# Sliding-window attention with a spectral mix on one core: the last rows of Yw and the jobs under the last loads

## The chip, the core and the metric

The kernel runs on one core of a Trainium2 chip. The metric is the device time of one execution in microseconds (us). The engines are PE (TensorE; PEld is its weight load), DVE (VectorE), ACT (ScalarE), POOL (GpSimd) and SP (SyncE), which only issues transfers here. SPq, ACTq and POOLq are the queues of an engine that issues a transfer.

## What is computed

Batch is 8, there are 8 heads of 64, 576 tokens, and a model width of 512. Attention looks back over 64 tokens; its result x then goes through a spectral mix: a real FFT over the tokens, two 512 x 512 matrices for each of the lowest 64 modes, the inverse FFT, a residual and a channel product with a relu.

```
x  = softmax(mask(q @ k.T / 8)) @ v            # heads side by side: [8, 576, 512]
X  = rfft(x, axis=1)                           # the first 64 modes are kept
Yr = Xr @ w_r[m] - Xi @ w_i[m]
Yi = Xr @ w_i[m] + Xi @ w_r[m]                 # for each mode m
u  = x + irfft(Y)
out = u + max(u @ w_ch, 0)                     # float32
```

## The kernel before

**Stages.** First comes attention, batch by batch, with the forward transform as matmuls (XQ holds the spectra). Meanwhile POOL already issues the loads of the 64 modes' matrices, 512 KB each, which run until about 398 us. The modes are worked off in groups of four (`mode_half`, L167 to L185: half of the input width, w_r or w_i). Each group gives rows of Y, which are turned so that they lie in `Yall` (128 rows: 64 real, 64 imaginary; 8 batches; 512 columns).

**The algebra of the end.** u is x plus the inverse transform of Y, and u @ w_ch is x @ w_ch plus the inverse transform of Y @ w_ch. So two tables of rows are kept: `Yall` (Y, bfloat16) and `Zall` (Yw = Y @ w_ch, fp32r). Each output tile of 128 tokens and 512 columns needs u, from x and a matmul of the table `trigI` with `Yall` (`yrows(b)`), and z, from `XW` = x @ w_ch and a matmul of `trigIr` with `Zall` (`zrows(b)`). There are 36 tiles: four per batch in `x_sb` (stored as [128, 2 halves, batch, 4 tiles, 256]) and four in `x4`, each of which joins the last 64 tokens of two batches and is sent as two outputs of 64 partitions.

**Jobs under the loads.** `jobs` is a list of pairs (prepare, done). `advance()` (L607) runs the next job's prepare and then the done of the job before it. The main loop (L807 to L863) runs one `mode_half`, then as many jobs as a count `want` allows; in the last halves these are 24 jobs spread over six halves. Before the last half but one it drains the list (L827). `batch_job(b)` (L670) turns the rows of a batch (DVE L673, PE L676, ACT L677) and multiplies them by `wch` (PE L604), and DVE casts the result to `zrows(b)` (L681). `early_job(b, c)` (L687), for the first four batches (NLB = 4) and each of their four tiles, adds z of the rows known so far into `XW` (PE L693, DVE L694) and makes an early sum of u called `UE`: for odd c in a spare place of XQ, by DVE (L698, L700); for even c in the place of x itself, by ACT (L702, L703, L705). The order of the jobs is a batch, its four tiles in the order 1, 0, 3, 2, the next batch, and at the end the four batches that have no early sums.

**The last rows.** The last two groups of modes (`LAST`, 16 rows) come after the early sums. Their rows of Y and Yw go two ways: as `YL` and `ZL`, small operands that are added onto the early sums (`late_u`, `late_z`, L752 to L764), and through `yst` and `zst` by SP's queue into `Yall` and `Zall` (L884, L895), for all tiles without early sums.

**The outputs.** `seq` (L728 to L734) is a list of 18 pairs of tiles. The eight AA pairs have early sums: PE adds XW and the late rows, DVE adds the late u (`take_u`, L775), ACT takes the relu (L781), POOL adds the two (L782), and the tile is sent. The ten BB pairs (`full`, L785) have none: PE adds x by an identity matmul (L789) and the rows of `Yall` (L740), ACT copies u (L792), PE does the same for z (L746, L740), and DVE takes the relu and adds (L796). The order is three AA pairs, then BB and AA in turn, then the rest of BB; the first two BB pairs are x4 tiles. Even and odd places of `seq` use different PSUM banks. The results lie in `ut`, a ring of seven pairs. `send` (L766) issues the outputs on SP's queue in the order of the program, with every other one on ACT's queue in the last two pairs.

```
banks_u(0); late_u(0); take_u(0)
pz = ...                                  # L890: the last rows of Y times wch
late_z(0); take_z(0)                      # sends the outputs of pair 0
nc.vector.tensor_copy(out=zst, in_=pz)
nc.sync.dma_start(out=Zall...[rows], in_=zst...)
```

Of the kernel before, what the change touches and what calls it, by code (L numbers as in the profile page):

```python
# [9 lines left out]
FP32 = mybir.dt.float32  # L10
# [16 lines left out]
def kernel(  # L27
# [163 lines left out]
    with tc.manual_schedule():  # L191
# [478 lines left out]
        def batch_job(b):  # L670
            def prepare():
                tr = trpool.tile([128, NDCH, 128], FP32R, name="tr")
                nc.vector.tensor_copy(out=tr, in_=YT[:, b])  # L673
                pt = bank("t", [128, NDCH, 128], BF16, "ptx")
                for c in range(NDCH):
                    nc.tensor.transpose(out=pt[:, c, :], in_=YT[:, b, c, :], identity=ident_bf)  # L676
                nc.scalar.copy(out=yrows(b), in_=pt.rearrange("p c e -> p (c e)"))  # L677
                return tr

            def done(tr):  # L680
                nc.vector.tensor_copy(out=zrows(b), in_=multiply(tr))  # L681

            jobs.append((prepare, done))

        UE = {}

        def early_job(b, c):  # L687
            i = 9 * (b // 2) + 4 * (b % 2) + c
            tokens = slice(128 * c, 128 * c + 128)

            def done(_):
                pz = bank("z")
                nc.tensor.matmul(out=pz, lhsT=trigIr[:, tokens], rhs=zrows(b), start=True, stop=True)  # L693
                nc.vector.tensor_tensor(out=XW[i], in0=pz, in1=XW[i].bitcast(FP32), op=ALU.add)  # L694
                pu = bank("t")
                halves = pu.rearrange("p (h e) -> p h e", h=2)
                if c % 2:
                    nc.tensor.matmul(out=pu, lhsT=trigI[:, tokens], rhs=yrows(b), start=True, stop=True)  # L698
                    UE[i] = spare[2 * b + c // 2].rearrange("p (h e) -> p h e", h=2)
                    nc.vector.tensor_tensor(out=UE[i], in0=halves, in1=tiles[i][0], op=ALU.add)  # L700
                else:
                    nc.tensor.matmul(out=halves, lhsT=ident_bf, rhs=tiles[i][0], start=True, stop=False)  # L702
                    nc.tensor.matmul(out=pu, lhsT=trigI[:, tokens], rhs=yrows(b), start=False, stop=True)  # L703
                    UE[i] = x_sb[:, :, b, c:c + 2, :].rearrange("p h c e -> p h (c e)").bitcast(FP32)
                    nc.scalar.copy(out=UE[i], in_=halves)  # L705

            jobs.append((lambda: None, done))


        tiles = []  # L710
        for kk in range(B // 2):
            for b in (2 * kk, 2 * kk + 1):
                tiles += [(x_sb[:, :, b, c, :], [(128 * c, b)], [out[b, 128 * c:128 * c + 128, :]]) for c in range(NTC - 1)]
            tiles.append((x4[:, :, kk, :], [(576, 2 * kk), (512, 2 * kk + 1)], [out[2 * kk + i, 512:576, :] for i in range(2)]))
        NT = len(tiles)
        XW = {}

        def x_jobs(pl, lo, hi):
# [9 lines left out]
        AA = [(18 * k // 2 + c, 18 * k // 2 + 4 + c) for k in range(NLB // 2) for c in range(4)]  # L728
        BB = [(8, 17), (26, 35)] + [(i, i + 1) for k in range(NLB // 2, B // 2) for i in range(9 * k, 9 * k + 8, 2)]
        assert sorted(i for p in AA + BB for i in p) == list(range(NT))  # L730
        seq = [AA.pop(0) for _ in range(3)]
        while AA:
            seq += [BB.pop(0), AA.pop(0)]
        seq += BB  # L734
# [37 lines left out]

        def take_u(n):
            for i in seq[n]:
                nc.vector.tensor_tensor(out=UE[i], in0=pu[i].rearrange("p (h e) -> p h e", h=2), in1=UE[i], op=ALU.add)  # L775

        def take_z(n):
            ut = ringA.tile([128, 2, DM], FP32, name="ut", tag="wt")
            for j, i in enumerate(seq[n]):
                rt = ut[:, j].rearrange("p (h e) -> p h e", h=2)  # L780
                nc.scalar.activation(out=ut[:, j], in_=ps[i], func=ACT_F.Relu)  # L781
                nc.gpsimd.tensor_tensor(out=rt, in0=UE[i], in1=rt, op=ALU.add)  # L782
                send(i, ut[:, j], n)

        def full(n):  # L785
            banks_u(n)
            ut = ringA.tile([128, 2, DM], FP32, name="ut", tag="wt")
            for j, i in enumerate(seq[n]):
                nc.tensor.matmul(out=pu[i].rearrange("p (h e) -> p h e", h=2), lhsT=ident_bf, rhs=tiles[i][0],  # L789
                                 start=True, stop=False)  # L790
                add_rows(pu[i], i, trigI, yrows, False)
                nc.scalar.copy(out=ut[:, j], in_=pu[i])  # L792
            tail_xw(n)
            for j, i in enumerate(seq[n]):
                add_rows(ps[i], i, trigIr, zrows, False)
                nc.vector.scalar_tensor_tensor(out=ut[:, j], in0=ps[i], scalar=0.0, in1=ut[:, j],  # L796
                                               op0=ALU.max, op1=ALU.add)
                send(i, ut[:, j], n)
# [8 lines left out]
        for i, (grp, hb) in enumerate(steps[EARLY:]):  # L807
            f, l = grp < EARLY or hb == 0, hb == 1
            if i == EARLY:
                while tables:  # L810
                    tables.pop(0)()
                while jobs or pend:
                    advance()
                close(stmp2, yp, ringB)
                Zall = pool("zall", side="right").tile([2 * NM, B, DM], FP32R, name="Zall")
                x_jobs(pool("xp1", side="right", reuse_waits="tile"), NX0, NT)
                nc.vector.memset(YT[:, :, :, rows], 0.0)
                nc.vector.tensor_scalar(out=trz.rearrange("p c g k -> p c (g k)"), scalar1=0.0, scalar2=None, op0=ALU.mult,
                                        in0=ident.unsqueeze(1).to_broadcast([128, NDCH, 128]))
                for g in range(4):  # L820
                    nc.sync.dma_start(out=trigL[32 * g:32 * g + 16], in_=trigI[rows, 0:512])
                    nc.sync.dma_start(out=trigLr.bitcast(FP32)[32 * g:32 * g + 16], in_=trigIr.bitcast(FP32)[rows, 0:512])
                given = 0
            if f:
                psm = bank("m")
            for ri in range(2):
                if half == n0 + n1 - 2:  # L827
                    while jobs or pend:
                        advance()
                if half == n0 + n1 - 1:  # L830
                    late["warm"], late["zeros"] = bank("z"), trigI[:, 0:DM]
                    keep_warm(5)
                    late["first"] = bank("z")
                    late[0][1]()
                    tail_xw(0)
                mode_half(psm, grp, hb, ri, f, l)
                load_weights(len(wlist))
                while ready:
                    ready.pop(0)()
                for t in tables[0:2]:  # L840
                    t()
                del tables[0:2]
                if half == 0:
                    nc.gpsimd.dma_start(out=wch, in_=moe_w_ch.rearrange("(c p) e -> p c e", p=128))
                if l and ri:
                    finish_group(grp, psm)
                    if grp == NGRP - 1:
                        ready.pop(0)()
                        for b in range(B):
                            batch_job(b)  # L850
                            if b < NLB:
                                for c in (1, 0, 3, 2):
                                    early_job(b, c)
                half += 1
                if half <= n0:
                    want = max(half - 4, 0) * NX0 // (n0 - 4)
                elif half <= n0 + n1 - 8:
                    want = (half - n0) * (NT - NX0) // (n1 - 8)
                else:
                    want = NT - NX0 + (half - n0 - n1 + 8) * (B + 4 * NLB) // 6  # L860
                while given < want:
                    advance()
                    given += 1  # L863
# [12 lines left out]
        for c in range(NDCH):  # L876
            nc.tensor.matmul(out=zl, lhsT=trz[:, c].rearrange("p g k -> p (g k)"), rhs=wch[:, c, :],
                             start=(c == 0), stop=(c == NDCH - 1))
        put_y()
        take()  # L880
        nc.vector.tensor_copy(out=ZL, in_=zl)
        yst = rowpool.tile([128, DM], BF16, name="yst")
        nc.scalar.copy(out=yst, in_=late["py"])
        nc.sync.dma_start(out=Yall[rows], in_=yst)  # L884
        banks_u(0)
        late_u(0)
        take_u(0)
        pz = bank("p")
        for c in range(NDCH):
            nc.tensor.matmul(out=pz, lhsT=tr[:, c, :], rhs=wch[:, c, :], start=(c == 0), stop=(c == NDCH - 1))  # L890
        zst = trpool.tile([128, NDCH, 128], FP32R, name="tr").rearrange("p c k -> p (c k)")
        late_z(0)
        take_z(0)
        nc.vector.tensor_copy(out=zst, in_=pz)
        nc.sync.dma_start(out=Zall.bitcast(FP32)[rows], in_=zst.bitcast(FP32))  # L895
        for n in range(1, len(seq)):
            if seq[n][0] in UE:
                tail_xw(n)
# [39 lines left out]
```

## Time and profile before

| | |
|---|---|
| runs shown | 448.43 us median of 3 (448.31 to 448.49) |
| the profiled execution | 448.99 us, of which the span from the first to the last instruction is 447.2 us |
| busy, share of the span | PE 76%, DVE 53%, PEld 48%, ACT 40%, POOL 32% |
| loads of the weights | 82 MB on POOL's queue, 211 GB/s |
| outputs | 38 on SP's queue and 2 on ACT's; 256 KB each, eight of them 128 KB |
| tail (last weights landed to the end) | about 398 to 447.2 us |

Three things help to read it. A share of busy time is a mean over stages with different limits; what a change in one stage is worth is read from that stage. The page's second part cuts the span into 40 slices of 11.2 us, each digit a busy share in tenths, and gives the clock that PE was granted and what the transfers moved. The line of an instruction in the order of time ends with how long its engine had been idle before it, and what ended that.

### The profile page before, as it was taken

How to read it: one execution, taken by the hardware profiler on the slowest of the kernel's cores; microseconds unless marked ns; L12 is line 12 of the kernel's file. 1: busy time of each engine (PE TensorE's matmuls, PEld its weight loads, DVE VectorE, ACT ScalarE, POOL GpSimd, SP SyncE). 2: the span in 40 equal slices, each digit the busy share in tenths (PEclk: the TensorE clock that was granted, in tenths of full speed). 3: DMA queues.
4: the chain of work that ended last, by engine and by line, in shares of the span. 5: the costliest groups of instructions: out<-in, count | busy, mean ns of one | idle time of the engine just before them, and what ended most of it. 6: DMA issues, size and time to landing. Idle time of an engine off the chain costs nothing. (4 is left out here: it accounts for less than half of the span.)

```text
span 447.2 us, 11052 instructions
## 1 busy us (share of the span) xinstructions
PE 337.8 (76%) x4720; PEld 214.0 (48%) x4765; DVE 234.9 (53%) x476; ACT 176.8 (40%) x315; POOL 142.9 (32%) x211
## 2 busy tenths in 40 slices
PE   6888899998999978974254565576866688796885
PEld 3666767676667665641032232343433343343443
DVE  8688787876676754863022111131322158735475
ACT  5665757575757563522001011121222122314363
POOL 9332323333233233232322322222232223106460
PEclk9999999999999998986569676798899899999799
DMA  8999999999999999999999999999999999933787
GB/s 203 210 212 210 211 211 210 211 211 213 210 211 211 211 211 210 211 211 211 235 233 218 211 211 211 211 211 211 211 211 211 211 211 211 211 65 99 210 292 282
DMA packets 48129, 93.65 MB, mean 209 GB/s; under 512 B 3664, under 2 KB 3856, under 8 KB 48080
## 3 DMA queue, kind: packets, MB, share of 16 engines
q0 software_dynamic: 42000, 81.73, 96.9%
q1 hardware_dynamic: 5792, 10.69, 7.3%
q8 instruction: 37, 0.61, 0.5%
q10 hardware_dynamic: 288, 0.52, 0.3%
q14 instruction: 12, 0.10, 0.1%
HBM read 163.58 MB, written 9.44 MB: 387 GB/s over the span
## 5 line engine op out<-in xcount | busy, mean ns | idle before, releaser
L158 POOL DMA_DIRECT2D wi<-in_moe_w_i_dram x62 | 44.0, 710 | 96.6 <-PE psm L178 41.3
L722 DVE CAST xw<-psz 128x512 fp32r<-128x512 f32 x36 | 24.9, 691 | 87.5 <-PE psz L604 84.6
L604 PE MATMUL psz<-wch,tr 128*128 128x512 f32 x176 | 59.1, 466 | 11.0 <-DMA wch<-in_moe_w_ch_dram 11.0
L158 POOL DMA_DIRECT2D wr<-in_moe_w_r_dram x53 | 37.8, 714 | 88.5 <-PE psm L178 40.2
L276 DVE TENSOR_REDUCE mx<-s 128x4 fp32r<-128x512 f32 x72 | 49.5, 688 | 26.3 <-PE s L272 26.0
L578 ACT CAST tr<-ptx 128x512 fp32r<-128x512 bf16 x36 | 21.1, 587 | 100.7 <-PE ptx L597 100.7
L178 PEld LDWEIGHTS <-XQ 128*32 128x32 bf16 x448 | 20.7, 166 | 77.0 <-issue 69.0
L178 PE MATMUL psm<-wi,XQ 128*32 128x512 bf16 x212 | 28.3, 461 | 31.1 <-DMA wi<-in_moe_w_i_dram 30.8
L286 ACT ACTIVATE p<-s 128x512 bf16<-128x512 f32 x72 | 39.7, 603 | 12.9 <-PE s L284 12.9
L604 PEld LDWEIGHTS psz<-wch,tr 128*128 128x128 f32 x176 | 34.9, 220 | 17.5 <-issue 11.5
L178 PE MATMUL psm<-wr,XQ 128*32 128x512 bf16 x180 | 25.1, 482 | 22.8 <-DMA wr<-in_moe_w_r_dram 22.8
L272 PE MATMUL s<-kT,qT 64*64 64x128 bf16 (+1 forms) x576 | 29.1, 221 | 6.7 <-issue 6.7
L229 ACT COPY kT<-tr 128x576 bf16<-128x576 bf16 x32 | 23.1, 723 | 24.4 <-PE tr L225 24.3
L295 DVE COPY pts<-pt 128x1024 bf16<-128x1024 bf16 (+1 forms) x40 | 25.2, 630 | 8.6 <-PE pt L292 7.3
L229 ACT COPY qT<-tr 128x576 bf16<-128x576 bf16 x32 | 23.3, 728 | 10.4 <-PE tr L225 10.4
L272 PEld LDWEIGHTS <-qT 64*64 64x64 bf16 x576 | 17.8, 107 | 18.0 <-issue 17.5
L284 PE MATMUL s<-mx,ident_r 128*128 128x512 f32 x72 | 26.2, 437 | 0.0
L229 ACT COPY vT<-tr 128x576 bf16<-128x576 bf16 x32 | 23.3, 727 | 4.1 <-PE tr L225 4.0
L292 PE MATMUL pt<-ident_bf,p 128*128 128x128 bf16 x288 | 23.8, 223 | 1.3 <-issue 1.1
L623 DVE TENSOR_TENSOR stg<-psm,Ypair 128x512 bf16<-128x512 f32 x10 | 6.9, 689 | 32.4 <-PE psm L178 32.4
L324 DVE TENSOR_TENSOR x_sb<-o,r 128x512 bf16<-128x512 f32 x32 | 22.1, 691 | 1.1
L225 PE MATMUL tr<-ident_bf,rawk 64*64 64x64 bf16 x576 | 15.4, 196 | 6.2 <-DMA rawk<-in_k_dram 4.8
(194 smaller groups left out, 604.0 us busy)
## 6 DMA issues: line engine op xcount, KB each, us to landing
wi<-in_moe_w_i_dram POOLq DMA_DIRECT2D x60, 512.0 KB, 15.9
wr<-in_moe_w_r_dram POOLq DMA_DIRECT2D x53, 512.0 KB, 16.2
out_dram<-ut SPq DMA_DIRECT2D x30, 256.0 KB, 2.3
rawv<-in_v_dram POOLq DMA_DIRECT2D x16, 288.0 KB, 14.8
rawk<-in_k_dram POOLq DMA_DIRECT2D x15, 288.0 KB, 15.1
rawq<-in_q_dram POOLq DMA_DIRECT2D x15, 288.0 KB, 14.1
Ypair<-in_moe_w_r_dram POOLq DMA_DIRECT2D x5, 512.0 KB, 15.1
x_sb<-in_moe_w_r_dram POOLq DMA_DIRECT2D x4, 512.0 KB, 15.3
```

Source lines behind the costliest of these rows:

```text
L158: nc.gpsimd.dma_start(out=w[:, 0:len(ps)], in_=src[ps[0]:ps[-1] + 1, HALF * hb:HALF * hb + HALF, :].rearrange("g (p j) e -> p g j e", j=NJ))
L178: nc.tensor.matmul(out=psm[32 * g:32 * g + 32, :], lhsT=of.rearrange("k s b m -> k (s b) m")[:, (3 * j + 1 - ri) * B:(3 * j + 5 - ri) * B, ...
L229: nc.scalar.copy(out=to, in_=pt.rearrange("p j n -> p n j"))
L272: nc.tensor.matmul(out=s[ro, t, lo:128], lhsT=lq, rhs=kT[ro, 64 * n - 64 + lo:64 * n + 64], start=False, stop=True, skip_group_check=True)
L276: nc.vector.tensor_reduce(out=mx, in_=s, axis=AX.X, op=ALU.max, negate=True)
L284: nc.tensor.matmul(out=s, lhsT=ident_r, rhs=mx.unsqueeze(2).to_broadcast([128, 4, 128]), start=False, stop=True, skip_group_check=True)
L286: nc.scalar.activation(out=p[:, 4 * c2:4 * c2 + 4, :], in_=s, func=ACT_F.Exp, scale=EX_SCALE)
L292: nc.tensor.transpose(out=pt[:, t, :], in_=st[u]["p"][:, t, :], identity=ident_bf)
L295: nc.vector.tensor_copy(out=ps[:, 0:nt, :], in_=pt[:, 0:nt, :])
L324: nc.vector.tensor_tensor(out=xo.rearrange("p c (h d) -> p c h d", d=64), in0=ov[:, :, :, 0:64], in1=rb, op=ALU.mult)
L604: nc.tensor.matmul(out=pz, lhsT=tr[:, c, :], rhs=wch[:, c, :], start=(c == 0), stop=(c == NDCH - 1))
L722: nc.vector.tensor_copy(out=XW[i], in_=multiply(tr))
```

## The change

It has four parts.

1. **Jobs.** The cast to `zrows(b)` goes from DVE to ACT. `early_job` is split in two kinds: `add_late(b, c)` (z into XW) and `early_u(b, cs)` (the early sum of u). Per batch these are seven jobs, in the order u of tile 1, z of 0, u of 3, z of 1, z of 2, u of 0 and 2 together, z of 3. They are queued behind the batch job of the next batch. So 36 jobs are spread over the six halves.
2. **Early sums in rows of their own.** For tiles 0 and 2 `UE` lies in one half of the batch's place in `x_sb` (one contiguous stretch of 512 float32), no longer in two tiles of both halves. The adds that use UE take it flat.
3. **x by halves.** `full` adds the rows of `Yall` first, and then x by two identity matmuls of 256 columns, one for each half.
4. **The last rows of Yw.** put_y comes behind the cast of ZL in the program, the product with wch (`pz`) ahead of `late_u(0)`; `late_z(0)` ahead of the copy to `zst`, which goes from DVE to ACT; and its transfer to `Zall` ahead of `take_u(0)` and `take_z(0)`, and so of every output. `seq` starts with four AA pairs and not three.

```
             def done(tr):
-                nc.vector.tensor_copy(out=zrows(b), in_=multiply(tr))
+                nc.scalar.copy(out=zrows(b), in_=multiply(tr))
...
-        def early_job(b, c):
...
+        def add_late(b, c):
             def done(_):
+                i = tile_of(b, c)
                 pz = bank("z")
+                nc.tensor.matmul(out=pz, lhsT=trigIr[:, 128 * c:128 * c + 128], rhs=zrows(b), start=True, stop=True)
                 nc.vector.tensor_tensor(out=XW[i], in0=pz, in1=XW[i].bitcast(FP32), op=ALU.add)
             jobs.append((lambda: None, done))
+
+        def early_u(b, cs):
+            def done(_):
+                pus = [bank("t") for _ in cs]
+                for c, pu in zip(cs, pus):
+                    i = tile_of(b, c)
+                    halves = pu.rearrange("p (h e) -> p h e", h=2)
+                    if c % 2 == 0:
+                        nc.tensor.matmul(out=halves, lhsT=ident_bf, rhs=tiles[i][0], start=True, stop=False)
+                    nc.tensor.matmul(out=pu, lhsT=trigI[:, 128 * c:128 * c + 128], rhs=yrows(b), start=(c % 2 == 1),
+                                     stop=True)
+                for c, pu in zip(cs, pus):
+                    i = tile_of(b, c)
+                    if c % 2:
+                        UE[i] = spare[2 * b + c // 2]
+                        nc.vector.tensor_tensor(out=UE[i].rearrange("p (h e) -> p h e", h=2),
+                                                in0=pu.rearrange("p (h e) -> p h e", h=2), in1=tiles[i][0], op=ALU.add)
+                    else:
+                        UE[i] = x_sb[:, c // 2, b].rearrange("p c e -> p (c e)").bitcast(FP32)
+                        nc.scalar.copy(out=UE[i], in_=pu)
+            jobs.append((lambda: None, done))
+
+        def early_jobs(b):
+            early_u(b, (1,))
+            add_late(b, 0)
+            early_u(b, (3,))
+            add_late(b, 1)
+            add_late(b, 2)
+            early_u(b, (0, 2))
+            add_late(b, 3)
...
-        seq = [AA.pop(0) for _ in range(3)]
+        seq = [AA.pop(0) for _ in range(4)]
...
-                nc.tensor.matmul(out=pu[i].rearrange("p (h e) -> p h e", h=2), lhsT=ident_bf, rhs=tiles[i][0],
-                                 start=True, stop=False)
-                add_rows(pu[i], i, trigI, yrows, False)
+                add_rows(pu[i], i, trigI, yrows, True)
+                for h in range(2):
+                    nc.tensor.matmul(out=pu[i][:, HALF * h:HALF * h + HALF], lhsT=ident_bf, rhs=tiles[i][0][:, h],
+                                     start=False, stop=True, skip_group_check=True)
...
                         for b in range(B):
                             batch_job(b)
-                            if b < NLB:
-                                for c in (1, 0, 3, 2):
-                                    early_job(b, c)
+                            if 0 < b <= NLB:
+                                early_jobs(b - 1)
...
-                    want = NT - NX0 + (half - n0 - n1 + 8) * (B + 4 * NLB) // 6
+                    want = NT - NX0 + (half - n0 - n1 + 8) * (B + 7 * NLB) // 6
...
-        put_y()
         take()
         nc.vector.tensor_copy(out=ZL, in_=zl)
+        put_y()
         yst = rowpool.tile([128, DM], BF16, name="yst")
         nc.scalar.copy(out=yst, in_=late["py"])
         nc.sync.dma_start(out=Yall[rows], in_=yst)
-        banks_u(0)
-        late_u(0)
-        take_u(0)
         pz = bank("p")
         for c in range(NDCH):
             nc.tensor.matmul(out=pz, lhsT=tr[:, c, :], rhs=wch[:, c, :], start=(c == 0), stop=(c == NDCH - 1))
+        banks_u(0)
+        late_u(0)
+        late_z(0)
         zst = trpool.tile([128, NDCH, 128], FP32R, name="tr").rearrange("p c k -> p (c k)")
-        late_z(0)
+        nc.scalar.copy(out=zst, in_=pz)
+        nc.sync.dma_start(out=Zall.bitcast(FP32)[rows], in_=zst.bitcast(FP32))
+        take_u(0)
         take_z(0)
-        nc.vector.tensor_copy(out=zst, in_=pz)
-        nc.sync.dma_start(out=Zall.bitcast(FP32)[rows], in_=zst.bitcast(FP32))
```

More of the change, by code (lines that the diff above doesn't have):

```diff
@@ L680, in done @@
             def done(tr):
-                nc.vector.tensor_copy(out=zrows(b), in_=multiply(tr))
+                nc.scalar.copy(out=zrows(b), in_=multiply(tr))
             jobs.append((prepare, done))
         UE = {}
-        def early_job(b, c):
-            i = 9 * (b // 2) + 4 * (b % 2) + c
-            tokens = slice(128 * c, 128 * c + 128)
+        def add_late(b, c):
             def done(_):
+                i = tile_of(b, c)
                 pz = bank("z")
-                nc.tensor.matmul(out=pz, lhsT=trigIr[:, tokens], rhs=zrows(b), start=True, stop=True)
+                nc.tensor.matmul(out=pz, lhsT=trigIr[:, 128 * c:128 * c + 128], rhs=zrows(b), start=True, stop=True)
@@ L694, in done @@
                 nc.vector.tensor_tensor(out=XW[i], in0=pz, in1=XW[i].bitcast(FP32), op=ALU.add)
[L695 to L705, printed above, removed]
@@ L715, with tile_of @@
         NT = len(tiles)
+        def tile_of(b, c):
+            return 9 * (b // 2) + 4 * (b % 2) + c
         XW = {}
@@ L774, in take_u @@
             for i in seq[n]:
-                nc.vector.tensor_tensor(out=UE[i], in0=pu[i].rearrange("p (h e) -> p h e", h=2), in1=UE[i], op=ALU.add)
+                nc.vector.tensor_tensor(out=UE[i], in0=pu[i], in1=UE[i], op=ALU.add)
         def take_z(n):
@@ L779, in take_z @@
             for j, i in enumerate(seq[n]):
-                rt = ut[:, j].rearrange("p (h e) -> p h e", h=2)
                 nc.scalar.activation(out=ut[:, j], in_=ps[i], func=ACT_F.Relu)
-                nc.gpsimd.tensor_tensor(out=rt, in0=UE[i], in1=rt, op=ALU.add)
+                nc.gpsimd.tensor_tensor(out=ut[:, j], in0=UE[i], in1=ut[:, j], op=ALU.add)
                 send(i, ut[:, j], n)
```

## The prediction

> **What bounds the kernel now.** I read the page's slices first, then the busy time of the engines per stretch of the end, the waits from 380 us on, the order of time there, and last the chain.
>
> ```profile
> span 447.2 us, 11052 instructions
> ...
> PE   6888899998999978974254565576866688796885
> ...
> PEclk9999999999999998986569676798899899999799
> ...
> GB/s 203 210 212 210 211 211 210 211 211 213 210 211 211 211 211 210 211 211 211 235 233 218 211 211 211 211 211 211 211 211 211 211 211 211 211 65 99 210 292 282
> ```
>
> Until slice 35 (about 391 us) the weights stream at 211 GB/s without a gap: nothing that only shortens work under them is worth its length. Behind them comes a tail of some 47 us. Its stretches (columns: length, busy us and count of PE, PEld, DVE, ACT, POOL; granted clock; DMA share; GB/s):
>
> ```profile
> 408.00:410.00 2.00, 1.95 (x11) 0.89 (x8) 1.61 (x3) 2.00 (x5) 2.00 (x3) 1.00 0.35 131
> 410.00:412.00 2.00, 0.15 (x1) 0.00 (x0) 0.00 (x0) 0.37 (x1) 2.00 (x3) 1.00 0.66 196
> 412.00:414.00 2.00, 0.00 (x0) 0.00 (x0) 0.00 (x0) 0.00 (x0) 2.00 (x2) 0.57 1.05 222
> 414.00:416.00 2.00, 1.67 (x4) 1.38 (x5) 0.36 (x1) 0.00 (x0) 0.24 (x1) 0.50 0.95 365
> 416.00:418.00 2.00, 2.00 (x8) 0.82 (x8) 1.20 (x3) 0.00 (x0) 0.00 (x0) 0.50 0.24 53
> ...
> 417.60:420.20 2.60, 2.60 (x12) 1.19 (x9) 1.29 (x2) 1.89 (x4) 1.51 (x2) 0.71 0.91 195
> 422.80:425.20 2.40, 1.70 (x8) 1.18 (x9) 0.65 (x2) 1.57 (x4) 2.22 (x2) 1.00 0.96 206
> 438.00:444.00 6.00, 4.62 (x20) 2.67 (x19) 4.27 (x7) 3.01 (x6) 0.00 (x0) 1.00 1.03 381
> ```
>
> PE stops at 410.15, its clock halves, and it comes back at half clock until 419. The waits and the order of time name the causes:
>
> ```profile
> PE psz L740 <- DMA Zall<-tr: 4.2, 1, 4.2
> ...
> PE psy L789 <- DVE x_sb L775: 2.8, 2, 1.5
> ```
>
> ```profile
> 406.82 2.52 POOL L782 TENSOR_TENSOR ut<-x_sb,ut 128x512 f32<-128x512 f32 x2 [21.48 <-ACT ut L781]
> ...
> 410.06 0.59 SPq L895 DMA_DIRECT2D Zall<-tr  x1
> ...
> 414.33 2.07 PE L740 MATMUL psz<-Zall,trigIr 128*128 128x512 f32 x4 [4.18 <-DMA Zall<-tr]
> ```
>
> The last rows of Yw (Zall) stand in SP's queue behind the first two outputs, which wait for POOL. The second wait is of another kind: L789 reads x of batches 4 to 7, L775 writes UE in batches 0 to 3; nothing is shared but the interval from one half of x_sb to the other. It occurs behind the two L775 that write x_sb (423.50, 430.67) and behind none that writes XQ, so I take it as false. The chain begins with that very wait and then runs through PE:
>
> ```profile
> 430.02 0.61 DVE x_sb L775
> 430.63 0.05 issue
> 430.68 0.39 PE psy L789
> ```
>
> Before the tail, under the loads, the batch jobs go round from cast to cast of Zall in 6.12 us, and end at the last L178 but one:
>
> ```profile
> 366.10 0.69 DVE L681 CAST Zall<-psz 128x512 fp32r<-128x512 f32 x1 [0.25 <-PE psz L604]
> ...
> 372.22 0.69 DVE L681 CAST Zall<-psz 128x512 fp32r<-128x512 f32 x1 [0.69 <-PE psz L604]
> ...
> 395.93 0.66 PE L178 MATMUL psm<-wr,XL 128*32 128x512 bf16 x8
> ```
>
> **Step 1: jobs under the last loads.** Their end (395.93) decides when the tail starts: the last four loads land at 393.0, 395.4, 396.7 and 398.0 (issue plus time to landing) and are used 2.6 to 3.0 us later. So at most 2.6 us can be won here; every us lost counts whole. Now a round is: cast 0.69, z matmul to its add 0.53, five DVE adds 0.61 apart (3.05), L673 0.41, multiply to cast 1.23: 5.9, measured 6.12. After: the cast is on ACT and batch b's adds come behind the multiply of b+1, so none waits for a fresh cast: multiply 1.02 on PE, first u matmul to add 0.41, five adds 3.05, L673 0.41: 4.9. Three rounds save 3.1. Against it: PE's slack shrinks, and of the three half-modes that fall in these rounds (each 0.38 issue and 0.59 work) I let two stand on the path, 1.9. Net **-1.2**. ACT's eight casts (L578, the same form, 587 ns: 4.7 us) lie in its idle time: ACT is busy some 9 of 33 us here, and if L677 delayed them all, 0.6 a round, the gain would be gone. More jobs per half (6 for 4) are the same instructions, cut finer. Bounds of the step: -2.6 to +1.0.
>
> **Step 2: Zall ahead.** Times on the old clock. put_y ends at 404.05, the four L890 matmuls (1.20) at 405.25, ACT's copy (0.58, behind yst, which ended at 404.85) at 405.9, SP issues at once, ahead of any output. Landing lies between that of Yall's rows (3.1 us) and the old one behind outputs (4.2): 409.1 to 410.2. take_u(0) starts 1.3 us later on DVE, at 405.9, since late_u follows L890; but POOL needs the relu too, which ends at 406.75 as before, and DVE's first add ends at 406.6. POOL still starts at 406.8: the first output does not move. PE then has three more AA pairs, 1.05 us each beside ACT's relus, to 409.2, then the first BB pair (x4): u matmuls 1.3, xw 0.47, first use of Zall at 411.0. **No wait**: 4.2 us off PE, and no idle stretch long enough for the clock to fall (4.8 us of work at 0.50, worth 2.4).
>
> **Step 3: x by halves, UE in rows of its own.** The two false waits held PE 1.27 and 1.50 us idle. One 512-column matmul becomes two of 256, on 20 tiles. The trace has none of 256; four transposes of 128 take 0.23, a 512 takes 0.22, so in proportion nothing, and at worst one uncovered weight load of 0.10 a tile, 2.0 in all. I take nothing: PE will not be last. A flat UE costs the same (POOL: 1270 ns for the x_sb form, 1280 for XQ).
>
> **PE's end.** First BB pair to 411.9; four AA at 1.25, 5.0; the second x4 pair 2.7; eight BB at 1.80 (434.99 to 436.79 is one): 14.4. It ends at 434.0, before at 442.67; with the 4.5 us from there to the span's end, 438.5.
>
> **What is late next: the outputs.** SP sends in the order of the program, so BB0 leaves behind AA3, and AA's outputs come from POOL at 1.26 each, now without a break from 406.82: AA3's first at 415.6. From there 26 full outputs and 8 half ones are left. Full ones moved at 381 GB/s (438 to 444): 0.69 each, 17.9. Half ones (64 partitions, 128 KB) moved 512 KB in 2.5 us in both stretches shown (195 and 206 GB/s at a full DMA share): 0.63 each, 5.0. POOL and PE supply four in 2.5 and 3.0 us, DMA needs 2.8 and for an x4 pair more, so it hardly pauses. Last landing 415.6 + 2.0 + 22.9 - 0.7 = 439.9, and 1.2 to the span's end as before: 441.1. That is later than PE's 438.5, so the tail wins **6.1**, not 8.7. [...]
>
> **Sum.** Span 447.2 - 1.2 - 6.1 = 439.9. The profiled execution took 448.99 with 1.79 outside its span, and lies 0.56 above the median 448.43: 448.43 - 7.3 = **441.1**.
>
> **Rivals.**
> - *Outputs do not bind* (0.18): the half outputs overlap others, PE's end decides, and the jobs gain all of 2.6: 448.4 - 8.7 - 2.6 = 437.1, up to 439.5. For it: POOL may pull outputs apart less than I think. Against: the two stretches at a full share.
> - *Jobs end no earlier or 1 us later*, outputs as forecast (0.14): 442.3 to 443.3. For it: DVE is busy 8.4 of the 11 us from 380, and half-modes now meet a PE with less slack.
> - *It doesn't do what it says* (0.10): Zall lands as late as before, 414.3, so PE waits 3.3 and runs at half clock again (2.4): PE's end 444.2 with the span's rest, so 3.0 and the 1.2 are won, 444.2; with no gain under the loads 445.4. If only the false waits stayed, PE would end 2.8 later, 441.3, beside the outputs, and nothing would show.
> - *Slower: the jobs turn serial* (0.04). Each single job now makes its round PE to DVE alone; if the two z banks and two t banks made each wait for the add before it, 28 jobs at 0.53 + 0.69 are 34, eight batches at 1.8 another 14, six half-modes 6: 54 for today's 32. The median would be 448.4 - 6.1 + 22 = 464. It decides from 6.1/28 = 0.22 us a job on. Against: adds now run 0.60 apart while matmuls of other banks go on.
> - *Slower: the clock* (0.02). PE's 28 us of tail work lose 1 us for each us of work at 0.50; 2.6 are covered by the outputs, so from 2.6 + 7.3 = 9.9 us of work on it is slower, up to 466. For it: the clock fell 2.4 us into the one long idle stretch. Against: it stayed at 1.00 through 420 to 446, with idle gaps of 1.3 and 1.5. [...]
>
> **Numbers.** Forecast 0.52 (439.7 to 442.3), the rivals as given. The range 437.4 to 444.8 leaves out the slow cases, the worst of the third and the edge of the first. 0.2% (0.9 us) is about what can be told from no change: faster 0.92, within 0.02 (the third at its worst), slower 0.06.
>
> **What would show it.** No wait of L740 on Zall, and SP's issue of Zall ahead of all L771; clock 1.00 from 408 to the end; no wait of L789's successor on L775; POOL busy without a break for 20 us; DMA share near 1 from 416 to 440, PE done 5 to 7 us before the span's end; the last L178 1 us earlier. Wrong would be: a PE that is still last, gaps in the outputs behind 418, or a last L178 later than 401.

## The result, and the profile after

The changed kernel takes 442.44 us (median of 4 runs, 442.31 to 442.64); the kernel before, run beside it, takes 448.37 (448.25 to 448.49). The ratio is 0.9868, with an interval of 0.9851 to 0.9885. The forecast was 441.1, in a range of 437.4 to 444.8.

The profiled execution took 442.31 us, 1.81 of them outside its span. Its page again has one column per slice, now of 11.0 us:

```profile
span 440.5 us, 11084 instructions
...
PE   6888899898999996986336565767766789799992
...
PEclk8899999999999996988559556788898989999997
...
GB/s 202 211 211 211 212 211 211 212 209 211 211 211 212 210 211 211 211 211 211 213 256 214 214 211 210 211 211 212 211 212 211 211 212 210 211 173 39 217 329 317
```

Two things differ from before. The last two slices move 329 and 317 GB/s, where before they moved 292 and 282 while PE was at work to the end. And PE's row ends in a 2, where it ended in a 5. The stretches of the tail show it at a finer grain (columns as before: length, busy us and count of PE, PEld, DVE, ACT, POOL; granted clock; DMA share; GB/s):

```profile
408.00:410.00 2.00, 1.95 (x14) 1.33 (x12) 1.64 (x3) 1.99 (x5) 2.00 (x3) 1.00 0.85 245
410.00:412.00 2.00, 2.00 (x12) 1.11 (x11) 1.42 (x3) 0.35 (x2) 2.00 (x3) 1.00 0.60 221
412.00:414.00 2.00, 2.00 (x12) 1.45 (x11) 1.06 (x2) 1.94 (x4) 2.00 (x2) 1.00 0.49 180
...
424.00:438.00 14.00, 8.14 (x44) 5.11 (x42) 6.78 (x11) 5.38 (x10) 1.59 (x2) 0.88 1.03 382
...
434.00:436.00 2.00, 0.00 (x0) 0.00 (x0) 0.00 (x0) 0.00 (x0) 0.00 (x0) 0.67 1.04 383
...
438.00:440.00 2.00, 0.00 (x0) 0.00 (x0) 0.00 (x0) 0.00 (x0) 0.00 (x0) 0.50 0.32 121
```

From 408 to 414 PE is busy 5.95 of 6 us at a clock of 1.00, where before it stood still from 410.15. From 424 to 438 the transfers have a share of 1.03 at 382 GB/s while PE does its last 8 us of work; from 434 no engine computes and the transfers run on at 383. The clock of 0.50 at the very end costs nothing, since PE has no work left. The order of time has the rows that the steps turn on:

```profile
394.98 0.66 PE L178 MATMUL psm<-wr,XL 128*32 128x512 bf16 x8
...
405.11 0.57 SPq L914 DMA_DIRECT2D Zall<-tr  x1
...
405.67 2.53 POOL L803 TENSOR_TENSOR ut<-x_sb,ut 128x512 f32<-128x512 f32 x2 [20.62 <-ACT ut L802]
...
409.86 1.09 PE L762 MATMUL pst<-Zall,trigIr 128*128 128x512 f32 x4
...
431.51 0.63 PE L762 MATMUL psz<-Zall,trigIr 128*128 128x512 f32 x2
```

Zall's transfer is issued at 405.11, ahead of every output, and lands 4.4 us later, at 409.5. The first matmul that reads it starts at 409.86 and has no bracket: it waited for nothing. PE ends at 432.14, 8.4 us before the span's end. No wait of PE on Zall and none of L812 (the x matmuls) on L797 (`take_u`) is in the list of waits any more. So the mechanism is the forecast one. What is to be tested is whether the outputs really set the end, which of the four parts brought the time, and why it is 1.3 us more than forecast.

### The profile page after: what moved, and what is told of

The parts are those of the page before. It is cut to its first block, busy times and chain, and to the rows that moved or that the text cites. A ratio compares the mean times of both kernels' runs of the same rounds, so it can differ in the third digit from the quotient of the medians.

```text
span 440.5 us, 11084 instructions
## 1 busy us (share of the span) xinstructions
PE 344.0 (78%) x4742; PEld 220.2 (50%) x4785; DVE 229.3 (52%) x467; ACT 181.4 (41%) x324; POOL 142.9 (32%) x211
## 4 chain that ended last, share of the span: by engine, by line
DMA 44%; PE 38%; issue 9%; ACT 4%; DVE 2%; POOL 1%; DVEq 0%; ACTq 0%; POOLq 0%
DMA wi<-in_moe_w_i_dram 33%; PE tr L225 6%; PE s L272 5%; DMA Yall<-in_moe_w_i_dram 4%; DMA rawk<-in_k_dram 4%; PE pt L292 4%; PE s L284 3%; PE vb L237 3%; DMA wr<-in_moe_w_r_dram 3%; PE psm L178 3%; PE o L312 2%; PE s L264 2%; PE psz L768 1%; PE psm L762 1%; PE pst L768 1%
## 5 line engine op out<-in xcount | busy, mean ns | idle before, releaser
L604 PE MATMUL psz<-wch,tr 128*128 128x512 f32 x176 | 62.7, 489 | 11.0 <-DMA wch<-in_moe_w_ch_dram 11.0
L178 PEld LDWEIGHTS <-XQ 128*32 128x32 bf16 x448 | 20.5, 167 | 69.6 <-issue 62.0
L178 PE MATMUL psm<-wi,XQ 128*32 128x512 bf16 x212 | 30.1, 479 | 28.8 <-DMA wi<-in_moe_w_i_dram 28.8
L604 PEld LDWEIGHTS psz<-wch,tr 128*128 128x128 f32 x176 | 37.7, 236 | 17.9 <-issue 11.3
L178 PE MATMUL psm<-wr,XQ 128*32 128x512 bf16 x180 | 24.8, 491 | 17.3 <-DMA wr<-in_moe_w_r_dram 16.6
L237 PE MATMUL vb<-ident_bf,vT 128*128 128x128 bf16 (+1 forms) x160 | 18.8, 230 | 1.3 <-PE o L312 0.7
```

Of the source, the lines that this page charges most:

```text
L178: nc.tensor.matmul(out=psm[32 * g:32 * g + 32, :], lhsT=of.rearrange("k s b m -> k (s b) m")[:, (3 * j + 1 - ri) * B:(3 * j + 5 - ri) * B, ...
L237: nc.tensor.transpose(out=pt[0:n, c].rearrange("p h d -> p (h d)"), in_=t[:, 128 * c:128 * c + n], identity=ident_bf)
```

## Experiments

Each edit is made to the changed kernel. The theory called A in the expectations is the prediction's: the outputs, which SP sends in the order of the program and which POOL's adds release, set the end, so PE has room to spare. Its main rival is that PE's waits still set it. The kernel before was run beside each experiment, and its median was 448.41 to 449.27 us there; so ratios compare better than times. As the mark to compare with, the changed kernel has 0.9868 and a span of 440.5.

**1. Zall behind the first outputs again.** Only the place of the copy and of the transfer is undone.

```
-        nc.scalar.copy(out=zst, in_=pz)
-        nc.sync.dma_start(out=Zall...[rows], in_=zst...)
         take_u(0)
         take_z(0)
+        nc.vector.tensor_copy(out=zst, in_=pz)
+        nc.sync.dma_start(out=Zall...[rows], in_=zst...)
```

> The changed kernel, but the copy to zst (on DVE again) and its transfer to Zall stand behind take_z(0), so behind the first two outputs, as before the change. Theory A (the outputs bind the tail: from AA3's first output on, the transfers have no room to spare, and PE is done 5 to 7 us early): PE waits about 3 us for Zall at its first use and perhaps runs at half clock behind that, but BB0's outputs cannot leave before AA3's anyway; 442.4 to 443.9 us, and the transfers near a full share from 418 on as in the changed kernel. Theory B (the tail is as long as PE's work and waits, as the prediction priced step 2 on PE): 3 us of wait and some 2.4 of half clock come back whole, 447 to 448 us.

442.71 us (442.14 to 445.04), ratio 0.9886 [0.9852, 0.9920], span 440.4. A wait for Zall is back, 0.9 us at the weight load where some 3 were expected, and so is the half clock; first a line of its waits (total, times, longest), then three us of its stretches:

```profile
PEld pst L762 <- DMA Zall<-tr: 0.9, 1, 0.9
```

```profile
409.00:412.00 3.00, 2.78 (x11) 1.55 (x10) 1.29 (x3) 1.92 (x5) 3.00 (x3) 0.50 0.89 184
```

The half clock (408.8 to 412.2) is not the wait's doing. It begins ahead of it, behind a pause in which PE waited for DVE's copy to `zst`:

```profile
406.30 0.37 PE L778 MATMUL psp<-stg,trigL 16*128 16x512 bf16 x1 [0.89 <-DVE tr L915]
```

PE ends at 435.1 instead of 432.1, and the span is the same (its jobs ended 0.4 us earlier; from the start of the last L178 but one to the span's end it takes 45.8 us, the changed kernel 45.5). So in the profiled execution three us of PE's time are worth at most 0.3: A. Two of the four runs took longer (443.24 and 445.04 us) and have no profile; why is open.

**2. x whole, early sums across both halves.** Parts 2 and 3 of the change are undone.

```
-                add_rows(pu[i], i, trigI, yrows, True)
-                for h in range(2):
-                    nc.tensor.matmul(out=pu[i][:, HALF * h:HALF * h + HALF], lhsT=ident_bf, ...)
+                nc.tensor.matmul(out=pu[i]..., lhsT=ident_bf, rhs=tiles[i][0], start=True, stop=False)
+                add_rows(pu[i], i, trigI, yrows, False)
```

> The changed kernel with UE in two tiles of both halves again, and x read whole by one identity matmul ahead of the rows of Yall: parts 2 and 3 of the change undone. Both theories see the false wait come back, but only at one place, since with four AA pairs ahead only the fourth BB pair stands right behind an add that writes x_sb: 1.3 to 1.8 us of idle PE. Theory A (outputs bind): 442.4 us, within 0.4. Theory B (PE binds): 443.7 to 445.2 us.

442.56 us (441.98 to 443.53), ratio 0.9868 [0.9848, 0.9888], span 440.7. Its list of waits has the old line again, under its new numbers:

```profile
PE psm L811 <- DVE x_sb L797: 1.5, 1, 1.5
```

The edit touches nothing but where x and UE lie and how they are read, and the wait comes and goes with it. The add reads the banks psy and psp there and the matmul writes psm, so it isn't a wait for a bank either, and the prediction's reading of it as a false one holds. That an interval which spans both halves is behind it stays the author's reading: which of the two parts removes it was not separated. The time is the same: A again.

**3. Three AA pairs first, not four.**

```
-        seq = [AA.pop(0) for _ in range(4)]
+        seq = [AA.pop(0) for _ in range(3)]
```

> The changed kernel with three AA pairs ahead and not four. Theory A (outputs bind, and POOL's adds hold the first of them back, 1.26 us a tile): BB0's outputs may leave behind AA2's, 2.5 us earlier, so the transfers reach a full share earlier; PE waits less than 1 us for Zall (landed 409.5, used at some 408.8). 441.0 to 442.0 us. Theory C (the fourth pair is needed to cover Zall's transfer): the wait counts, 443 us or more.

441.49 us (441.28 to 441.80), ratio 0.9842 [0.9826, 0.9858], span 439.5: 1.0 us less. PE now waits 0.2 us for Zall, but the outputs run closer together. The same three us in the changed kernel and in this one:

```profile
414.00:417.00 3.00, 3.00 (x18) 1.91 (x17) 2.48 (x4) 1.37 (x3) 3.00 (x4) 1.00 0.63 237
```

```profile
414.00:417.00 3.00, 3.00 (x18) 1.90 (x18) 2.48 (x4) 1.62 (x4) 2.57 (x3) 1.00 0.94 242
```

With four AA pairs ahead the transfers are busy 0.63 of this stretch, with three 0.94: by the order of the program, the first BB pair's outputs, which need no POOL, leave one AA pair earlier. The bytes of these three us are nearly the same, since it is half outputs that leave there (in the kernel before they moved 195 and 206 GB/s at shares of 0.91 and 0.96); from 414 to 424 the one has moved 256 GB/s and the other 298. So the fourth pair ahead costs about a microsecond, and PE's short wait (0.2 us) cost nothing that shows.

**4. The second output of each x4 tile left out.**

```
-            for h, o in enumerate(to):
+            for h, o in enumerate(to[0:1]):
```

> The changed kernel without the second 64-row output of each of the four x4 tiles (four of the forty output transfers are left out, so half of the last 64 tokens' rows are not written). Theory A (outputs bind and a half output costs some 0.62 us of all transfers): 1.5 to 2.5 us less, 440.0 to 441.0 us. Theory B (PE binds) or half outputs that overlap others: no change, 442.2 to 442.5 us.

439.63 us (439.38 to 439.88), ratio 0.9800 [0.9784, 0.9816], span 438.1. All matmuls and adds are still done, PE ends at 432.2 as before the edit, and 2.4 us of the span are gone (2.8 by the medians, a little more than was expected), so the outputs do set the end. The four halves come to 0.6 to 0.7 us each, against the 0.63 of the sum.

**5. Only the jobs new.** Edits 1, 2 and 3 together: of the tail, only the product `pz` still comes ahead of `late_u(0)`.

> The changed kernel with the three parts of the tail undone together: Zall's copy and transfer behind the first outputs, UE and x as before, three AA pairs ahead (the product of the last rows with wch stays ahead of late_u). Only the jobs under the loads are new. Theory A (each part alone can be taken away because the outputs still bind, and together they are what made PE last): PE is last again, 446.8 to 447.8 us, with the wait of some 4 us on Zall, half clock and two false waits. Theory D (the tail's gain comes from something else than these three, for instance the product being earlier): 442 to 444 us.

446.73 us (ten runs, 445.33 to 448.49), ratio 0.9944 [0.9926, 0.9962], span 445.1. Both waits are there, the false ones in their old size and Zall's with 2.9 us for the 4.2 of before, and PE is at work until 440.5:

```profile
PE psz L762 <- DMA Zall<-tr: 2.9, 1, 2.9
PE psy L811 <- DVE x_sb L797: 2.8, 2, 1.5
```

```profile
438.00:440.00 2.00, 2.00 (x10) 1.21 (x10) 1.33 (x3) 0.62 (x2) 0.00 (x0) 1.00 1.03 381
```

Edits 1 and 2 cost next to no span and edit 3 gains when made alone; the three together lose 4.6 us of span between the profiled executions (3.4 us by the ratios). As long as two of the three stand, PE is early enough and the outputs are the later of the two.

**6 and 7. One part of the tail alone.** x_only keeps parts 2 and 3 (edits 1 and 3 made), z_only keeps part 4's transfer (edits 2 and 3 made).

> The changed kernel with Zall's transfer behind the first outputs and three AA pairs ahead, but with UE in rows of its own and x by halves: of the tail only parts 2 and 3 are new. Theory A: PE has the wait on Zall (4.2) and its half clock (2.4) but no false waits (2.8), so PE's end is 442.7 - 0.95 - 2.8 = 439.0 on the clock of before, 4.5 more to the end, against the outputs' end of some 439.5 to 440.5: PE and outputs both late, 443.5 to 445.5 us. If the false waits were hidden in the kernel before too: 446.8 to 447.8 us.

x_only: 443.29 us (443.04 to 444.59), ratio 0.9878 [0.9856, 0.9900], span 441.3, a little below what was expected. PE ends at 436.4, 4.9 us ahead of the span's end, nearly as close as in experiment 5 (4.6): PE and the outputs are both late.

> The changed kernel with three AA pairs ahead, and UE and x as before: of the tail only part 4 is new, Zall's transfer ahead of all outputs. Theory A: with three AA pairs both false waits are back (2.8 us of PE), PE's last matmul moves from 432.9 (three pairs ahead, x by halves) to 435.7, which with 4.5 more is 440.2, about the outputs' end; 441.3 to 442.6 us, so this part alone does all that the four do together. If parts 2 and 3 had a share of their own: 444 us or more.

z_only: 441.95 us (441.88 to 442.30), ratio 0.9855 [0.9842, 0.9869], span 440.1; both false waits are back (2.8 us) and PE ends at 435.5, 4.6 us ahead of the span's end. Sending Zall ahead is thus enough by itself for all that the tail's parts bring together; the other two alone bring 3.8 of the 4.6 us of span. Beside experiment 3, whose order of tiles both share, the false waits cost 0.6 us of span and Zall's old place 1.8. With four AA pairs first they cost 0.2 and nothing (experiments 2 and 1): that is what the fourth pair buys for its microsecond.

**8 and 9. The jobs.** cast_dve puts the cast back on DVE in the new order; jobs_own leaves it on ACT and queues a batch's early jobs behind its own batch job.

```
-                nc.scalar.copy(out=zrows(b), in_=multiply(tr))
+                nc.vector.tensor_copy(out=zrows(b), in_=multiply(tr))
```

```
-                            if 0 < b <= NLB:
-                                early_jobs(b - 1)
+                            if b < NLB:
+                                early_jobs(b)
```

> The changed kernel with the batch jobs' cast to zrows(b) on DVE again, in the new order of the jobs. Theory J (DVE's queue is on the path of the jobs, as the prediction has it: 0.61 for each of the four casts that fall among adds, some of it in DVE's pauses): the last half-mode but one (L178) starts 0.5 to 2.0 us later than 394.98, and the whole takes 442.9 to 444.4 us. Theory K (PE and the half-modes set the jobs' pace by now): no later, 442.2 to 442.7 us.

> The changed kernel with each batch's early jobs behind its own batch job and not behind the next one's, the cast still on ACT. Theory J (an add must not wait for a fresh cast: a round takes ACT's 0.59 and the wake of PE more): L178 starts 0.5 to 2.0 us later than 394.98, 442.9 to 444.4 us. Theory K: no later, 442.2 to 442.7 us.

cast_dve: 442.84 us (442.61 to 443.06), ratio 0.9862 [0.9845, 0.9879], span 441.2; its last L178 but one starts at 395.55. jobs_own: 443.21 us (442.65 to 443.32), ratio 0.9871 [0.9851, 0.9891], span 440.9; it starts at 395.32. The changed kernel has 394.98 and the one before 395.93. So by the start of that line the cast is worth 0.57 and the order 0.34. The eight profiles with the changed kernel's jobs untouched (its own and those of experiments 1, 3, 4, 6 and 10 to 12) have this start at 394.57 to 395.01, and both edits lie outside of that. From there to the span's end cast_dve takes 45.7 us, jobs_own 45.6 and the changed kernel 45.5, so what the jobs lose goes into the span whole. The ratios tell none of the three apart. In jobs_own the wait that the new order is to avoid can be seen, in its waits from 366 to 396:

```profile
PEld psz L691 <- ACT Zall L681: 2.2, 3, 0.7
```

In the changed kernel this line stands at 0.3 us. The two parts of step 1 work as thought. By one profile each they bring some 0.6 and 0.3 us, with a scatter of 0.4 in what they are compared with.

**10. Two of POOL's adds taken by DVE.** If POOL's 1.26 us per add hold the first outputs back, a faster relu and add should gain. For the second and fourth AA pair DVE does both in one instruction.

```
+                if n in (1, 3):
+                    nc.vector.scalar_tensor_tensor(out=ut[:, j], in0=ps[i], scalar=0.0, in1=UE[i],
+                                                   op0=ALU.max, op1=ALU.add)
+                    send(i, ut[:, j], n)
+                    continue
                 nc.scalar.activation(out=ut[:, j], in_=ps[i], func=ACT_F.Relu)
```

> The changed kernel; for the second and the fourth AA pair DVE takes the relu and adds UE in one instruction, and neither ACT nor POOL works on them. Theory A (outputs bind, and POOL's 1.26 us a tile holds back AA0 to AA3 and all that SP has queued behind them): AA1 leaves at about 408.4, AA3 and BB0 near 413 and not 415.7, the transfers reach a full share some 3 us earlier; 439.2 to 441.0 us. Theory E (DVE, with 1.3 us more per such pair, holds the PSUM banks longer and becomes what is late): no gain, 442.2 us or more.

441.35 us (five runs, 441.15 to 442.62), ratio 0.9839 [0.9825, 0.9852]. About 1.1 us are gained, less than forecast. The profile fell on the slowest of the five runs (442.62, span 440.8), so it shows what went wrong in that one. In the order of time, PE now waits for DVE, which has two pairs' work in a row; and in the stretches the clock falls just there:

```profile
407.69 1.39 PE L768 MATMUL psz<-xw,ident_r 128*128 128x512 f32 x2 [0.84 <-DVE ut L803]
```

```profile
407.00:408.00 1.00, 0.31 (x1) 0.19 (x1) 1.00 (x3) 0.97 (x2) 0.98 (x1) 1.00 1.03 129
408.00:409.00 1.00, 0.90 (x2) 0.29 (x1) 1.00 (x3) 0.00 (x0) 0.03 (x1) 0.59 0.90 238
409.00:415.00 6.00, 5.78 (x19) 3.65 (x20) 3.61 (x6) 1.17 (x2) 2.46 (x2) 0.50 0.82 301
415.00:416.00 1.00, 1.00 (x8) 0.39 (x7) 0.79 (x2) 0.00 (x0) 0.00 (x0) 1.00 0.04 8
```

One stretch with PE busy 0.31 of a microsecond is followed by nearly 7 us at 0.50; the BB pairs come late, and at 415 nothing is left to send (a share of 0.04). The direction is that of A. Its size isn't shown: the four other runs have spans of 439.4 to 439.6 us and no profile.

**11. The second halves on ACT's queue.**

```
-                by = nc.scalar if n >= len(seq) - 2 and (i + h) % 2 else nc.sync
+                by = nc.scalar if (h == 1 or n >= len(seq) - 2 and (i + h) % 2) else nc.sync
```

> The changed kernel; the second half (64 partitions) of each x4 tile is issued on ACT's queue and the first on SP's, so that both halves can be under way together. [...] If two such transfers only take turns (theory G): 442.2 to 442.7 us. [...]

440.86 us (440.64 to 441.71), ratio 0.9833 [0.9818, 0.9848], span 439.2: 1.6 us less, the fastest of all that write the whole result. The time lies below the range of theory G, but nothing in the rates speaks for two transfers side by side. The same ten us of the changed kernel and of this one:

```profile
411.00:421.00 10.00, 10.00 (x58) 6.01 (x56) 7.90 (x14) 6.16 (x12) 10.00 (x9) 1.00 0.72 227
```

```profile
411.00:421.00 10.00, 9.40 (x52) 5.61 (x51) 6.53 (x12) 5.68 (x12) 9.58 (x9) 1.00 0.88 274
```

Per unit of DMA share they move 227 / 0.72 = 315 and 274 / 0.88 = 311 GB/s, the same. But the transfers are busy 8.8 us of the ten instead of 7.2, which is about the gain (1.6 us by the medians, 1.3 of span). The halves leave at 411.15 and 415.83, while SP's queue still stands at an output that waits for POOL. As far as these means over full and half outputs can show it, the rate was no higher with the second queue, 311 against 315; the 1.6 us here were won by what the other queue had no need to wait for.

**12. Both halves on ACT's queue.** If leaving early is what counts, one other queue for both halves should do as well.

```
-                by = nc.scalar if n >= len(seq) - 2 and (i + h) % 2 else nc.sync
+                by = nc.scalar if (m == 64 or n >= len(seq) - 2 and (i + h) % 2) else nc.sync
```

> The changed kernel with both halves of every x4 tile issued on ACT's queue (in two_q it was the second halves alone, 440.9 us). In two_q the transfers moved no more per busy share than in the changed kernel (274 GB/s at 0.88 against 227 at 0.72 from 411 to 421, 311 to 315 per full share), but were busy 1.6 us longer by 421. Theory H (the gain comes from leaving earlier: on ACT's queue the halves are not held behind POOL's adds): both halves now leave early, busy share above 0.72 from 411 to 421 again, 439.8 to 440.9 us. Theory F (the gain comes from two queues working on different partitions at once): both halves stand in one queue again, so it is gone, 441.8 to 442.6 us. Against H counts that ACT waits for DVE ahead of each such transfer and may hold up relus (up to 0.6 us a pair).

443.75 us (443.39 to 446.33), ratio 0.9894 [0.9872, 0.9916], span 441.9: no gain, and no forecast met. First the same ten us, then ACT's order of time and the stretch behind it:

```profile
411.00:421.00 10.00, 7.22 (x37) 3.92 (x35) 4.47 (x8) 3.03 (x7) 7.35 (x7) 1.00 0.89 279
```

```profile
417.04 2.89 ACTq L793 DMA_DIRECT2D out_dram<-ut  x4
420.03 1.09 ACT L802 ACTIVATE ut<-psz 128x512 f32<-128x512 f32 x2 [3.52 <-DMA out_dram<-ut]
```

```profile
421.00:423.00 2.00, 2.00 (x11) 0.93 (x11) 1.38 (x3) 1.91 (x5) 2.00 (x2) 0.87 0.24 80
```

Until 421 the halves do leave early, from a single queue, with a share of 0.89 at 313 GB/s per unit: so what experiment 11 gained is in the earlier leaving, and needs no second queue beside it. Then it is given back. ACT issues four transfers in a row and stands idle 3.52 us ahead of its next relu; with no relu POOL has nothing to add, SP nothing to send, and the transfers fall to a share of 0.24. ACT, which also computes, pays here for what it issues.

## Why the prediction came out as it did

**What bounds the kernel.** Right. PE's two waits set the end of the kernel before: with both back (experiment 5) PE is again at work to within 4.6 us of the span's end.

**Step 1, jobs: -1.2 forecast, -0.95 by the start of the last L178 but one** (395.93 to 394.98), or -1.26 by the profile of experiment 5. The rounds from cast to cast did not shrink to 4.9 us: the casts start at 366.80 (two), 372.57, 380.01 and 387.49, with half-modes between them that wait for their weights (0.76 us at 383.20). PE had caught up with the loads in places, which the step had only as "PE's slack shrinks". In size the net came out right, its two terms (three rounds saved, two half-modes on the path) only in sum, and that they met it in sum is partly luck.

**Step 2, Zall ahead: right in what it does, wrong in one term.** No wait, clock 1.00 to the end of PE's work, first output not moved. The landing took 4.4 us and not 3.1 to 4.2, although only Yall's rows were ahead of it (the first outputs are issued from 406.98 on, while it is under way): the bound "behind outputs" was no upper bound. The slack to the first use was 0.35 us, and by the profiles of experiments 1 and 3 a small wait there would have cost next to nothing.

**Step 3, false waits and 256-column matmuls: right.** The waits went and came back with experiment 2. PE's end, forecast at 434.0 on the old clock, so 433.05 on the new one, was 432.14: matmuls of 256 columns cost nothing that shows (a BB pair takes PE 1.81 us in both kernels, from 437.78 to 439.59 before and from 427.34 to 429.15 after).

**What is late next: right, and the term that was mis-sized.** The outputs set the end (experiments 1 to 4). Span forecast 439.9, measured 440.5. Of the 0.6, 0.25 are step 1's. The other 0.35 belong to the tail, -5.75 for -6.1. The sum let the transfers run from AA3's first output without a pause (it "hardly pauses"); in fact AA3's outputs still came 1.26 us apart, and the share from 414 to 417 was 0.63, a pause of 1.1 us. Experiment 3 takes that pause away and gains 1.0. That the tail missed by 0.35 only, and not by 1.1, is partly luck: AA3's first output was ready at 414.4, some 0.3 ahead of the forecast 415.6 on the new clock (414.65), and the other 0.5 must be made up in the 23 us of outputs; where stays open.

**The sum.** The largest part of the miss, 0.7 us of 1.3, is in the last line. The forecast took 0.56 off because the profiled execution of before lay that much over its median. The changed kernel's lies 0.13 below its own. How far one execution lies from a median says nothing of the next kernel: from span to span the change is -6.7, where -7.3 was forecast.

**The rivals.** Zall landed at 409.5 and not at 414.3, which excludes that the change doesn't do what it says. "Outputs do not bind" is excluded by experiment 4, and by PE's end 8.4 us ahead. "Jobs end no earlier" (442.3 to 443.3) gives the measured time, but for the wrong reason: they do end earlier. "If only the false waits stayed … nothing would show" is what experiments 2 and 7 found. The rivals of serial jobs and of the clock did not occur; half clock during PE's work was seen in experiments 1, 5, 6 and 10, and in the profile of experiment 1 its 3.4 us left the end nearly where it was. The clock rival's reading that the clock fell 2.4 us into the idle stretch is off a little: PE stopped at 410.15 and the clock fell at 412.26, 2.1 us later.

**What it could have done better.** The fourth AA pair ahead was read as cover for Zall. The same row that prices it (POOL, 1.26 a tile) says that it also holds the first BB output back; by experiment 3 the change would have been faster without it. The fastest version run is experiment 11 (ratio 0.9833 [0.9818, 0.9848], against 0.9868 [0.9851, 0.9885] of the change). Its edit together with three AA pairs first wasn't tried.

## What to carry to other kernels

When a wait goes, price the next bound in its own currency: here bytes over 381 GB/s from the first output that leaves without a gap, and that sum was right to 0.35 us, in part by luck. Undo the parts of a change one at a time and all together: three parts that could each be undone for next to nothing cost 4.6 us of span when undone jointly, since any two of them kept PE ahead of the outputs. And look at the order in which one queue issues: here a transfer that was ready stood behind one that was not, and moving it to another queue gained 1.6 us in experiment 11 and nothing in experiment 12, where ACT issued four in a row and stood idle 3.52 us ahead of its next relu.

## What the runs showed of the hardware

- A transfer of 256 KB into 16 partitions of Zall took 4.4 us to land with one 128 KB transfer ahead of it (3.4 us), no faster than the 4.2 of before behind two outputs.
- The clock fell to 0.50 after pauses of PE of only 0.84 us (experiment 10), 0.89 us (experiment 1) and 0.9 us (x_only). Pauses of 1.27 and 1.50 us in the kernel before (up to 423.5 and 430.7) left it at 1.00, so the length of a pause doesn't decide alone; what does is not shown.
- The half clock lasted either 3.4 us (408.8 to 412.2 in experiment 1, 412.9 to 416.4 in experiment 5, 407.2 to 410.6 in x_only) or twice that (412.3 to 419.1 in the kernel before, 408.2 to 415.0 in experiment 10), with PE busy 5.78 of 6 us in the last of them (409 to 415).
- An output of 64 partitions and 128 KB costs about as much of the end as a full one of 256 KB (0.6 to 0.7 us by experiment 4, against 0.69).
